# Twelve subtractions moved from VectorE to GpSimd, and one change of issue order, in a spectral-mix kernel

## The chip, the core and the metric

The kernel runs on one core of a Trainium2 chip. The metric is the device time in microseconds (us). The engines are named as the profile names them: PE is TensorE (PEld its weight loads), DVE is VectorE, ACT is ScalarE, POOL is GpSimd, SP is SyncE, which here only issues DMAs. Each engine works through its own instructions in order and waits on semaphores for the others.

## What is computed

Two branches over a token axis of 4096 tokens, 640 channels and batch 2 are mixed by a gate per token: a Fourier branch (`A`) and a gated feed-forward network (`B`, 640 to 1728 to 640).

```python
g = sigmoid((x * gate_w).sum(-1, keepdims=True))
# A: real FFT over the tokens, then per frequency a complex two-layer network in 4 blocks of 160 channels
z = rfft2(x).reshape(B, H, Wf, 4, 160)
hr = relu(zr @ w1[0] - zi @ w1[1] + b1[0]);  hi = relu(zi @ w1[0] + zr @ w1[1] + b1[1])
or_ = hr @ w2[0] - hi @ w2[1] + b2[0];       oi_ = hi @ w2[0] + hr @ w2[1] + b2[1]
a = irfft2(softshrink(or_, 0.01) + 1j * softshrink(oi_, 0.01))
# B
b = (gelu(x @ w_gate) * (x @ w_up)) @ w_down
out = g * a + (1 - g) * b
```

All of it is float32.

## The kernel before

**Operands in two parts.** TensorE multiplies in the type float32r, so each operand is kept as a high part (ACT copies the float32 tile into a float32r tile, `high`, line 276) and a low part (the tile minus its high part, `low`, line 279, a subtraction on DVE unless another engine is given). `split` is the one after the other. A product then is three matmuls: high by high, low by high, high by low.

**Stages.** (1) Up to about 1380 us, three passes over groups of gate and up weight tiles (`groups`), each over 16 tiles of 512 tokens, called pairs (`keys`), compute the hidden layer. In a pair, `quad` saves products by sums of operands: of the four token blocks b11, b12, b21, b22 it also uses the differences t1 = b12 - b11, t2 = b22 - t1, t3 = b22 - b12 and t4 = b21 - t2. These are the tiles `xd`, made at line 441 by `x_prep`. In the first pass each difference is split and its two parts, the tile `xo`, are also stored to DRAM (`xD`) by a DMA that POOL issues at line 468, and the later passes load them. The first pair is made without differences (`plain`), and while TensorE computes it, ACT and DVE prepare the first four weight tiles (`w`, `wt`) and the operands of the second pair; while it computes the second, those of the third. So the second and the third pair are `keys[1]` and `keys[2]`. Small pieces of such preparation are handed out to numbered hooks between the matmul groups (`spread`, `slots`), and the places fix the order of each engine's instructions. The first Fourier step runs in between.

(2) From about 1380 to 1800 us, 64 steps (`steps`, S = 64), each one block of one chunk of frequencies. At a step i the loop issues `mlp1` of step i (first layer), `mlp2` of step i-1 (second layer), and the first inverse step `inv1` of step i-2 where that closes a pair of blocks. `mlp1` makes most of its output `h` at once and hands back a function, `rest_of`, for the last 32 channels (tiles `hl`, lines 926 to 928); the loop calls it, as `more`, behind `mlp2`. `mlp2` evicts its two PSUM banks with an ACT instruction into `m` (line 951) and a DVE instruction into `y` (line 952). `y_split` splits `y` into `ys`.

(3) From about 1800 us, 32 steps of the last inverse Fourier step (`inv2`) and of the down projection (`down`), which mixes and stores the output. The operands of `inv2` are loaded by `c_load` into `s2` and split by `c_split` into the tiles `s2s`; those of `down` are loaded by `h_load` into `hraw`, and `h_s3` subtracts two of them on POOL (line 1145).

**What orders the passage from (2) to (3).** The table `fin` lists what is issued at the end of each of the last steps of stage 2. At S-4 stands `c_load` of the first inverse operands, at S-2 the first `h_load`, and at S-1 `c_split(0)`, the first `h_op` and `h_s3`. At i = S, `mlp2` of the last step needs what `rest_of` made at S-1, and `inv2(0)` comes behind it.

The lines that the change and the prediction touch: 276 (high parts, ACT), 279 (low parts), 441 (differences), 468 (DMA of a difference's parts), 509 (copies out of PSUM in `quad`), 869 and 870 (high and low part of `h`), 909 (`kc`), 923, 926, 927 and 928 (the rest of the first layer), 951 and 952 (second layer out), 1145 (`h_s3`).

Of the kernel before, what the change touches and what calls it, by code (L numbers as in the profile page):

```python
# [213 lines left out]
def spectral_mix_kernel(ctx: ExitStack, tc: tile.TileContext, a):  # L214
    nc = tc.nc
# [26 lines left out]
    def small(shape, dt=F32, name="small"):  # L242
        return pool.tile(shape, dt, name=name, tag="small", bufs=18)
# [31 lines left out]
    def high(dst, src, scale=1.0):  # L275
        nc.scalar.activation(dst, src, AF.Copy, scale=scale)  # L276

    def low(dst, src, hi, eng=nc.vector):
        eng.tensor_sub(dst, src, hi.bitcast(F32))  # L279

    def split(dst_h, dst_l, src, eng=nc.vector):

        high(dst_h, src)
        low(dst_l, src, dst_h, eng)
# [8 lines left out]
    def mms(dst, ops):  # L293
        for i, (l, r) in enumerate(ops):
            nc.tensor.matmul(dst, l, r, start=i == 0, stop=i == len(ops) - 1)  # L295
# [130 lines left out]
    def x_prep(key, k, eng=nc.vector):  # L426

        name = XNAMES[k]
        kept = int(name[1]) - 1 if name in ("t1", "t2", "t3", "t4") else None

        def src():
            d = XT[key]
            if not made(key) and kept is not None:
                m = mid([P, 2, 512], F32R, name="xo")
                ld(m.rearrange("p h n -> p (h n)").bitcast(F32), xD[key[1]][:, kept])
                XO.setdefault(key, {})[name] = [m[:, h] for h in range(2)]
                return
            for n, p, q in (("t1", "b12", "b11"), ("t2", "b22", "t1"), ("t3", "b22", "b12"), ("t4", "b21", "t2")):
                if n not in d and (n == name or (n, name) == ("t1", "t2")):
                    d[n] = small([P, 512], name="xd")  # L440
                    nc.vector.tensor_sub(d[n], d[p], d[q])  # L441
            if name == "t5":
                d[name] = small([P, 256], name="xd")
                nc.vector.tensor_sub(d[name], d["k4"][:, :256], d["k4"][:, 256:])
            return d[name]

        def hi(copy=high):
            if not made(key) and kept is not None:
                return
            if name == "t5":  # L450
                if not T5:
                    T5.append(mid([P, 2, 2, 256], F32R, name="xo"))
                t = [T5[0][:, keys.index(key) % 2, h] for h in range(2)]
            else:
                m = mid([P, 2, 512], F32R, name="xo")
                t = [m[:, h] for h in range(2)]
                if kept is not None:
                    XM[key, name] = m
            XO.setdefault(key, {})[name] = t
            copy(t[0], XT[key][name])  # L460

        def lo():
            if not made(key) and kept is not None:
                return
            t = XO[key][name]
            low(t[1], XT[key][name], t[0], eng)
            if kept is not None:
                nc.gpsimd.dma_start(xD[key[1]][:, kept],
                                    XM.pop((key, name)).rearrange("p h n -> p (h n)").bitcast(F32))
        return [src, hi, lo]  # L470
# [401 lines left out]
    def mlp1(b, c, n, sums):  # L872
        F = width(b, c)
        z, (sh, sl) = Z.pop((b, c, n))
        w, wl = W1[n], W1L[n]
        t1, t2 = ZL1[b, c], ZL2[b, c]

        part = lambda k: (w[:, k:k + P], w[:, LOW1 + k:LOW1 + k + P])
        wl = wl.rearrange("p h c -> p (h c)")


        def group(dst, m):
            r = 1 - m
            wh, wlo = part(OUT1[m])
            mms(dst, [(wh, z[0][:, r]), (wh, z[1][:, r]), (wlo, z[0][:, r]),
                      (wl[:, P * m:P * m + P], t1[:, n, :F]), (wl[:t2.shape[0], 384 + P * m:512 + P * m], t2[:, n, :F])])

        def last(dst):

            for r in range(2):  # L890
                k = LAST1[r]
                nc.tensor.matmul(dst, w[:, k:k + P], z[0][:, r], start=r == 0, stop=False, skip_group_check=True)  # L892
                nc.tensor.matmul(dst, w[:, k:k + P], z[1][:, r], start=False, stop=False, skip_group_check=True)  # L893
            nc.tensor.matmul(dst, wl[:, 256:384], t1[:, n, :F], start=False, stop=True, skip_group_check=True)  # L894
        h = two(b, c, "h")
        if wide(b, c):
            if n < 2:
                x = small([P, 2, CW], F32R, name="hl")
                nc.gpsimd.memset(x[64:66, 1].bitcast(F32), 1.0)
                HW[n] = x[:, 0], x[:66, 1]  # L900
            hA, hB = HW[n % 2]
        else:
            hA, hB = hl1[n % 2], hl2[n % 2]
        H[b, c, n] = (h, hA, hB)
        pk = bank()
        wh, wlo = part(OUT1["k"])
        mms(pk[:, :F], [(wh, sh[:, :F]), (wh, sl[:, :F]), (wlo, sh[:, :F])])
        kc, hs = part_of(b, c, 1), (small if wide(b, c) else mid)([P, 2, F], name="hs")
        nc.scalar.activation(kc[:, :F], pk[:, :F], AF.Copy)
        pm = [bank()] * 2 if F == CH else [bank(), bank()]  # L910
        for r in range(2):
            d = pm[r][:, r * CH:(r + 1) * CH] if F == CH else pm[r][:, :F]
            group(d, r)
        for r in range(2):
            d = pm[r][:, r * CH:(r + 1) * CH] if F == CH else pm[r][:, :F]
            nc.vector.tensor_add(hs[:, r, :F], d, kc[:, :F])
        sums()
        relu_split(h[0], h[1], hs)
        pl = bank()
        last(pl[:, :F])  # L920
        hs = part_of(b, c, 2)[:64]
        nc.scalar.activation(hs, pl[64:, :F], AF.Copy)
        nc.vector.scalar_tensor_tensor(hs, pl[:64, :F], b1r[:, n:n + 1], hs, op0=OP.add, op1=OP.add)

        def rest_of():
            nc.scalar.activation(hB[:64, :F], hs, AF.Relu)
            nc.scalar.activation(hA[:64, :F], hs, AF.Relu)
            nc.vector.scalar_tensor_tensor(hA[64:, :F], hs, 0.0, hB[:64, :F].bitcast(F32), op0=OP.max,
                                           op1=OP.subtract)
        return rest_of  # L930
# [189 lines left out]
            ld(raw, dr(scr2[b], na * P * 2 * D + r * D, [[2 * D, P], [1, D]]))  # L1120
            S2[i].append(raw)

    def c_split(i):
        m = [mid([P, 1024], F32R, name="s2s") for k in range(3)]
        raws, S2[i] = S2[i], {}
        for n, k in enumerate((0, 2, 1, 3)):
            h, l = (m[e if n < 3 else 2][:, o:o + 320] for e, o in ((0, 16 + 320 * (n % 3)), (1, 352 if n > 2 else 32 + 320 * n)))
            split(h, l, raws[k // 2][:, 320 * (k % 2):320 * (k % 2) + 320])
            S2[i][k] = h, l

    def h_load(i, part):
# [179 lines left out]
    keys = [(gr, tp) for gr in range(3) for tp in ([1, 2, 3, 4, 0, *range(5, 16)] if gr == 1 else range(16))]  # L1311
# [76 lines left out]
    for k, (b, n2) in enumerate(a_seq):  # L1388
        i, j = steps_a[k]
# [31 lines left out]
    for i, key in enumerate(keys):  # L1421
# [16 lines left out]
        for j, t in enumerate(quads):  # L1438
# [10 lines left out]
            n = len(late)  # L1449
# [19 lines left out]
    S = len(steps)  # L1469
# [11 lines left out]
    def events(i, j):  # L1481
        for f, *args in todo.get((i, j), []):
            f(*args)
    wl = lambda part, *js: [(wd_load, j, part) for j in js]
# [6 lines left out]
           S - 5: wl(0, 3, 4, 5),  # L1491
           S - 4: [(c_load, 0), *wl(1, 0, 1)],
           S - 3: [(v_load, 1)],
           S - 2: [(h_load, 0, 0), *wl(1, 2), (h_load, 0, 1)],
           S - 1: [(c_split, 0), (h_op, 0, "a11"), *wl(1, 3, 4, 5), *wl(0, 6), (h_s3, 0, nc.gpsimd), (c_load, 1)],
           S: [(h_s2, 0), (h_op, 0, "s2"), (c_split, 1)],
           S + 1: [*wl(1, 6), *wl(3, 0, 3, 6), *wl(4, 4, 5), *wl(5, 4, 6), (wd_later,), (h_s1, 0)]}
    for i in range(S + 2):
        events(i, 0)
        flush()  # L1500
        if i < S:
            events(i, 1)
            if i + 1 < S:
                sums = main_z(*steps[i + 1]) if i else ahead_z
                if steps[i + 1][2] == 3:
                    sc_pop(*steps[i + 1][:2])
            more = mlp1(*steps[i], sums if i + 1 < S else lambda: None)
        if 0 <= i - 1 < S:
            mlp2(*steps[i - 1])
        if i < S:  # L1510
            more()
        if 0 <= i - 2 < S and steps[i - 2][2] % 2:
            inv1(steps[i - 2][0], steps[i - 2][1], steps[i - 2][2] // 2)
            if wide(*steps[i - 2][:2]) and steps[i - 2][2] == 3:
                HW.clear()
                WT.clear()
        if 0 <= i - 1 < S:
            b, c, n = steps[i - 1]
            if n % 2:
                y_split(b, c, n // 2)  # L1520
            if i == S:
                uu.update(inv2(0))
        for f, *args in fin.get(i, []):
            f(*args)
# [4 lines left out]
    for i in range(len(c_seq)):  # L1529
        n = i + 1 if i + 1 < len(c_seq) else None  # L1530
# [60 lines left out]
```

## Time and profile before

| | us |
|---|---|
| median of 3 runs (lowest, highest) | 2536.0 (2535.12, 2536.41) |
| the profiled execution's own time | 2535.42 |
| its span, first to last instruction | 2533.7 |
| PE busy | 2527.2 |
| DVE busy | 2052.9 |
| ACT busy | 1492.7 |
| POOL busy | 372.4 |

A row of a timeline reads: start in us from the span's start, length in us, engine, line, operation, output <- inputs by the program's names with buffer numbers left out, shapes, how many, and in brackets the idle time of the engine before it with what ended it. Equal instructions that follow each other are merged, and their times then overlap a little at the joints. The granted TensorE clock was 1.0 over the whole profiled execution.

### The profile page before, as it was taken

To read this page: it belongs to the slowest core of one execution; us is meant where nothing else is said; L and a number is where in the kernel's file an instruction comes from. 1 tells how busy PE (TensorE), PEld (TensorE's weight loads), DVE (VectorE), ACT (ScalarE), POOL (GpSimd) and SP (SyncE) were. 2 spreads that over 40 slices of the span, in tenths; PEclk is the share of its full clock that TensorE was granted. 3 is DMA by queue.
4 is the path that set the end of the run, shared out by engine and by line. 5 is a ranking of instruction groups with operands and counts; after the bars stand their busy time and mean duration, and the time that the engine had idled before them with its cause. 6 is when DMAs were issued, how large, how long until landed. Compare 5 with 4: busy or idle time off the path is not lost.

```text
span 2533.7 us, 54552 instructions
## 1 busy us (share of the span) xinstructions
PE 2527.2 (100%) x20299; PEld 2522.9 (100%) x20299; DVE 2052.9 (81%) x4218; ACT 1492.7 (59%) x3494; POOL 372.4 (15%) x379
## 2 busy tenths in 40 slices
PE   9999999999999999999999999999999999999999
PEld 9999999999999999999999999999999999999999
DVE  7878767777777767766667788888999999899998
ACT  6655555666665655655556788787644444444443
POOL 0000000000000000000003111111133333333332
PEclk9999999999999999999999999999999999999999
DMA  6566647676767677766767354548744444344432
GB/s 231 195 214 197 212 169 234 203 240 210 223 204 253 192 227 226 232 219 209 225 224 229 121 166 141 169 144 263 288 146 150 156 157 139 134 151 157 154 130 103
DMA packets 345982, 483.77 MB, mean 191 GB/s; under 512 B 24748, under 2 KB 221996, under 8 KB 345716
## 3 DMA queue, kind: packets, MB, share of 16 engines
q1 hardware_dynamic: 330884, 438.47, 54.2%
q0 software_dynamic: 14832, 41.82, 4.6%
q8 instruction: 160, 2.62, 0.4%
q14 instruction: 106, 0.87, 0.1%
HBM read 300.55 MB, written 179.64 MB: 190 GB/s over the span
## 4 chain that ended last, share of the span: by engine, by line
PE 96%; DVE 2%; DMA 1%; ACT 1%; issue 0%; SPq 0%; DVEq 0%; ACTq 0%
PE bank L483 54%; PE bank L1234 22%; PE bank L295 14%; PE bank L811 3%; PE bank L645 1%; PE bank L892 1%; PE bank L893 1%; DMA wraw<-in_wgu_dram 0%; DVE w L279 0%; DVE xo L279 0%; PE bank L894 0%; DVE xd L441 0%; DMA xraw<-in_xT_dram 0%; DVE uu L1239 0%; DVE h L554 0%
## 5 line engine op out<-in xcount | busy, mean ns | idle before, releaser
L483 PE MATMUL bank<-xo,w 128*128 128x256 f32 x11676 | 1351.0, 277 | 0.7 <-ACT u L509 0.6
L483 PEld LDWEIGHTS bank<-xo,w 128*128 128x128 f32 x11676 | 1342.2, 188 | 1.7 <-ACT u L509 1.3
L1234 PE MATMUL bank<-wx,ho 128*128 128x320 f32 x3844 | 560.6, 306 | 0.0
L1234 PEld LDWEIGHTS bank<-wx,ho 128*128 128x128 f32 x3844 | 557.1, 188 | 0.0
L509 ACT ACTIVATE u<-bank 128x256 f32<-128x256 f32 x408 | 156.6, 384 | 253.4 <-PE bank L483 248.3
L279 DVE TENSOR_TENSOR ho<-hraw,ho 128x640 fp32r<-128x640 f32 (+3 forms) x384 | 273.8, 754 | 21.4 <-ACT ho L276 18.4
L276 ACT ACTIVATE ho<-hraw 128x640 fp32r<-128x640 f32 x320 | 166.8, 571 | 91.5 <-PE bank L1234 66.0
L509 ACT ACTIVATE p<-bank 128x256 f32<-128x256 f32 x204 | 78.6, 385 | 148.4 <-PE bank L483 61.9
L279 DVE TENSOR_TENSOR xo<-xraw,xo 128x512 fp32r<-128x512 f32 x209 | 143.2, 686 | 23.9 <-ACT xo L276 23.2
L542 DVE TENSOR_TENSOR u<-bank,u 128x256 f32<-128x256 f32 x204 | 85.9, 421 | 89.2 <-ACT u L509 86.6
L279 DVE TENSOR_TENSOR xs<-xr,xs 64x640 fp32r<-64x640 f32 x128 | 104.9, 820 | 58.1 <-ACT xs L276 55.6
L295 PE MATMUL bank<-wm,h 128*128 128x320 f32 (+1 forms) x792 | 137.7, 309 | 0.0
L276 ACT ACTIVATE xo<-xraw 128x512 fp32r<-128x512 f32 x209 | 131.0, 627 | 6.1 <-DMA xraw<-in_xT_dram 4.3
L551 DVE TENSOR_TENSOR u<-bank,u 128x256 f32<-128x256 f32 x204 | 85.5, 419 | 60.0 <-PE bank L483 59.3
L647 DVE TENSOR_TENSOR as<-bank,as 64x320 f32<-64x320 f32 x256 | 113.7, 483 | 24.9 <-ACT as L646 23.7
L295 PEld LDWEIGHTS bank<-wm,h 128*128 128x128 f32 (+1 forms) x792 | 117.9, 185 | 1.4
L598 POOL MEMSET h<- 64x512 f32 x16 | 8.4, 522 | 749.8 <-PE bank L645 437.5
L483 PE MATMUL bank<-wx,ho 128*128 128x320 f32 x764 | 116.3, 307 | 0.0
L525 DVE TENSOR_TENSOR p<-bank,p 128x256 f32<-128x256 f32 x204 | 86.6, 424 | 36.5 <-PE bank L483 31.9
L483 PEld LDWEIGHTS bank<-wx,ho 128*128 128x128 f32 x764 | 112.1, 188 | 0.0
L276 ACT ACTIVATE ho<-hs 128x640 fp32r<-128x640 f32 (+1 forms) x128 | 69.0, 570 | 70.2 <-DVE ho L279 51.1
L646 ACT ACTIVATE as<-bank 64x320 f32<-64x320 f32 x256 | 96.8, 427 | 16.4 <-PE bank L645 13.9
(168 smaller groups left out, 3669.6 us busy)
## 6 DMA issues: line engine op xcount, KB each, us to landing
xo<-xD SPq DMA_DIRECT2D x124, 512.0 KB
xraw<-in_xT_dram SPq DMA_DIRECT2D x225, 256.0 KB
hD<-h SPq DMA_DIRECT2D x224, 256.0 KB
hraw<-hD SPq DMA_DIRECT2D x128, 320.0 KB
xD<-xo POOLq DMA_DIRECT2D x64, 512.0 KB, 4.3
sc<-scr SPq DMA_DIRECT2D x65, 320.0 KB
xr<-in_x_dram SPq DMA_DIRECT2D x64, 320.0 KB
scr<-as SPq DMA_DIRECT2D x64, 320.0 KB
```

Of the source, the lines that this page charges most:

```text
L276: nc.scalar.activation(dst, src, AF.Copy, scale=scale)
L279: eng.tensor_sub(dst, src, hi.bitcast(F32))
L295: nc.tensor.matmul(dst, l, r, start=i == 0, stop=i == len(ops) - 1)
L483: nc.tensor.matmul(dst, l, r, start=first and i == 0, stop=i == len(ops) - 1, skip_group_check=True)
L509: copy = lambda d, s_: nc.scalar.activation(d, s_, AF.Copy)
L525: nc.vector.tensor_add(p1, A, p1)
L542: nc.vector.tensor_add(u4, C, u4)
L551: nc.vector.tensor_add(u2, C, u2)
L646: nc.scalar.activation(stg[hi, cs], pa[lo, :320], AF.Copy)
L647: nc.vector.tensor_add(stg[hi, cs], pa[hi, :320], stg[hi, cs])
L811: nc.tensor.matmul(pz[:, kp * P:(kp + 1) * P], SC[b, c, kp][:, o:o + P], ft, start=True, stop=True)
L1234: nc.tensor.matmul((X, Y)[k], *op, start=n[k] == 0 and not (more and k), stop=n[k] == tot[k] - 1, skip_group_check=True)
```

## The change

Three edits. The differences t1 to t4 of the second and the third pair (eight subtractions of 128x512) are computed on POOL; their high and low parts stay on ACT and DVE. `c_split(0)` is issued one step earlier, at S-2 ahead of `h_load`, and its four low parts (128x320) are on POOL; its high parts stay on ACT. At step S-1 alone, the rest of the first layer is issued ahead of `mlp2`, and not behind it.

```diff
             for n, p, q in (("t1", "b12", "b11"), ("t2", "b22", "t1"), ("t3", "b22", "b12"), ("t4", "b21", "t2")):
                 if n not in d and (n == name or (n, name) == ("t1", "t2")):
                     d[n] = small([P, 512], name="xd")
-                    nc.vector.tensor_sub(d[n], d[p], d[q])
+                    (nc.gpsimd if key in keys[1:3] else nc.vector).tensor_sub(d[n], d[p], d[q])
...
-    def c_split(i):
+    def c_split(i, eng=nc.vector):
...
-            split(h, l, raws[k // 2][:, 320 * (k % 2):320 * (k % 2) + 320])
+            split(h, l, raws[k // 2][:, 320 * (k % 2):320 * (k % 2) + 320], eng)
...
-           S - 2: [(h_load, 0, 0), *wl(1, 2), (h_load, 0, 1)],
-           S - 1: [(c_split, 0), (h_op, 0, "a11"), *wl(1, 3, 4, 5), *wl(0, 6), (h_s3, 0, nc.gpsimd), (c_load, 1)],
+           S - 2: [(c_split, 0, nc.gpsimd), (h_load, 0, 0), *wl(1, 2), (h_load, 0, 1)],
+           S - 1: [(h_op, 0, "a11"), *wl(1, 3, 4, 5), *wl(0, 6), (h_s3, 0, nc.gpsimd), (c_load, 1)],
...
             more = mlp1(*steps[i], sums if i + 1 < S else lambda: None)
+        if i == S - 1:
+            more()
         if 0 <= i - 1 < S:
             mlp2(*steps[i - 1])
-        if i < S:
+        if i < S - 1:
             more()
```

On POOL at the start of the program, the subtractions come to stand between the DMAs that store the differences' parts. The rows with a minus are before, those with a plus are now.

```order
 L239 MEMSET gap 128x112
-L468 DMA xD_89<-xo 128x1024 x4
+L441 ISA
+L441 TENSOR_TENSOR xd<-xraw 128x512
+L468 DMA xD_89<-xo 128x1024
+L441 TENSOR_TENSOR xd<-xraw 128x512
+L441 TENSOR_TENSOR xd<-xraw,xd 128x512
+L468 DMA xD_89<-xo 128x1024 x2
+L441 TENSOR_TENSOR xd<-xraw,xd 128x512
+L468 DMA xD_89<-xo 128x1024
+L441 TENSOR_TENSOR xd<-xraw 128x512
```

The four differences of the second pair stand in the order t3, t1, t2, t4. Each DMA waits for a low part that DVE makes, so t1 and t2 now stand behind the storing of t3, and t4 behind that of t2 and t1. The first of the third pair follows the last DMA of the second.

On ACT at the end of stage 2, step S-1 before (the tiles: `kc` and `hs` of the first layer, `hl` its rest, `m` of the second layer, `is` of the first inverse step, `s2s` the first inverse operands):

```order
L909 ACTIVATE kc<-bank 128x256
L869 ACTIVATE h<-hs 128x512
L922 ACTIVATE hs<-bank 64x256
L951 ACTIVATE m<-bank,neg2lam 128x320 x2
L926 ACTIVATE hl_20268<-hs 64x256
L927 ACTIVATE hl_20267<-hs 64x256
L987 ACTIVATE is<-bank 128x320 x2
L276 ACTIVATE s2s<-s_26169 128x320
L276 ACTIVATE s2s<-s_26171 128x320
L276 ACTIVATE s2s<-s_26169 128x320
L276 ACTIVATE s2s<-s_26171 128x320
```

and with the change:

```order
L276 ACTIVATE s2s<-s_26169 128x320
L276 ACTIVATE s2s<-s_26171 128x320
L276 ACTIVATE s2s<-s_26169 128x320
L276 ACTIVATE s2s<-s_26171 128x320
L909 ACTIVATE kc<-bank 128x256
L869 ACTIVATE h<-hs 128x512
L922 ACTIVATE hs<-bank 64x256
L926 ACTIVATE hl_20268<-hs 64x256
L927 ACTIVATE hl_20267<-hs 64x256
L951 ACTIVATE m<-bank,neg2lam 128x320 x2
L987 ACTIVATE is<-bank 128x320 x2
```

The four high parts of `s2s` moved from behind the step's work to ahead of it, and the two `m` from ahead of the two `hl` to behind them.

On POOL at the same place, with the change:

```order
L1007 DMA v<-in_v_dram 128x256
L279 TENSOR_TENSOR s2s<-s_26169,s2s 128x320
L279 TENSOR_TENSOR s2s<-s_26171,s2s 128x320
L279 TENSOR_TENSOR s2s<-s_26169,s2s 128x320
L279 TENSOR_TENSOR s2s<-s_26171,s2s 128x320
L1145 TENSOR_TENSOR hraw<-hraw 128x640
L1145 TENSOR_TENSOR hraw<-hraw 128x256
```

The four low parts are new here. Before, `h_s3` (line 1145) followed the DMA directly.

## The prediction, made before the result was known

> **What bounds the kernel now.** I read the page's busy times first, then PE's waits, then the two places that the change touches.
>
> ```profile
> PE 2527.2 (100%) x20299; PEld 2522.9 (100%) x20299; DVE 2052.9 (81%) x4218; ACT 1492.7 (59%) x3494; POOL 372.4 (15%) x379
> PE bank L1344 <- DVE zero L1340: 1.2, 1, 1.2
> PE bank L295 <- ACT is L987: 0.7, 1, 0.7
> PE bank L483 <- ACT u L509: 0.6, 2, 0.5
> ```
>
> PE is busy for 2527.2 of 2533.7 us and all its waits add up to 2.5 us. The first lies at the very end, out of the change's reach; the second is the passage into the last stage, the third is in the start. The change removes no work from PE, so it can win only these small waits, and whatever it makes late on PE is paid in full. I look at the start.
>
> ```profile
> 18.00:57.00 39.00, 38.52 (x335) 38.10 (x335) 38.52 (x95) 23.63 (x62) 4.12 (x8) 1.00 0.59 186
> 18.00:57.00 39.00, 5.38 (x8) 1.00 0.59 186
> 18.00:57.00 39.00, 6.18 (x13) 1.00 0.59 186
> 66.80 21.56 PE bank L483 x190
> 13.85 38.09 PE L483 MATMUL bank<-xo,w 128*128 128x256 f32 x330
> 52.42 9.81 PE L483 MATMUL bank<-xo,w 128*128 128x256 f32 x84 [0.48 <-ACT u L509]
> ```
>
> The first three rows are the window from 18 to 57 us: all engines (PE, PEld, DVE, ACT, POOL), then line 441 alone (the eight subtractions, 0.67 us each), then DVE's operations that read a PSUM bank. DVE is as full as PE: 38.52 of 39 us. It is therefore a second bound, and a delay in its queue reaches PE. How much PE loses there: from 66.80 on, 190 matmuls take 21.56 us, 0.1135 each; at that rate 330 would take 37.45, and they took 38.09. With the 0.48 us idle before 52.42 the start costs PE **1.1 us**.
>
> ```profile
> 17.68 0.69 DVE L587 TENSOR_TENSOR h<-bank,gelu 128x512 f32<-128x512 f32 x1 [4.86 <-ACT gelu L586]
> 20.96 0.68 DVE L441 TENSOR_TENSOR xd<-xraw 128x512 f32<-128x512 f32 x1
> 21.56 0.42 DVE L339 TENSOR_TENSOR wt<-wraw 128x256 f32<-128x256 f32 x1
> 39.38 0.41 DVE L345 TENSOR_TENSOR wt<-wraw 128x256 f32<-128x256 f32 x1
> 50.74 0.69 DVE L441 TENSOR_TENSOR xd<-xraw,xd 128x512 f32<-128x512 f32 x1
> 39.83 1.34 ACT L276 ACTIVATE w<-wt 128x512 fp32r<-128x512 f32 x4 [1.05 <-DVE wt L345]
> 41.60 0.36 ACT L509 ACTIVATE p<-bank 128x256 f32<-128x256 f32 x1
> 51.46 0.63 ACT L276 ACTIVATE xo<-xd 128x512 fp32r<-128x512 f32 x1 [1.65 <-DVE xd L441]
> 52.00 0.37 ACT L509 ACTIVATE u<-bank 128x256 f32<-128x256 f32 x1
> ```
>
> The way from DVE to PE is seen twice. DVE's `wt` at 39.38 releases ACT's high parts at 39.83, behind which ACT's copy out of PSUM at 41.60 is queued. DVE's difference at 50.74 releases ACT's high part at 51.46, behind that stands the copy `u` at 52.00, and PE resumes at 52.42. Both times PE waits for a PSUM copy that stands on ACT behind an operand that DVE made late.
>
> **Edit 1, eight subtractions to POOL.** What leaves DVE: from 20.96 to the next start at 21.56, 0.60 us each. What comes to POOL has no row of its size; two neighbours:
>
> ```profile
> L712 POOL TENSOR_TENSOR raw<-raw 128x128 f32<-128x128 f32 x4 | 1.8, 456 | 2.3 <-DMA raw<-in_w1m_dram 2.2 <-PE bank L483 0.2
> L279 POOL TENSOR_TENSOR ys<-y,ys 128x640 fp32r<-128x640 f32 x29 | 45.7, 1576 | 316.4 <-ACT ys L276 285.6 <-issue 22.4 <-PE bank L295 8.5
> ```
>
> Between 0.456 us for 128 columns and 1.576 for 640, a line gives 1.30 for 512 and 0.88 for 320. Whether DVE goes on meanwhile is the question that decides; these rows of the last stage bear on it:
>
> ```profile
> 1856.36 1.15 DVE L279 TENSOR_TENSOR ho<-hraw,ho 128x640 fp32r<-128x640 f32 x2
> 1826.12 2.54 DVE L279 TENSOR_TENSOR ho<-hraw,ho 128x640 fp32r<-128x640 f32 x2 [0.33 <-ACT ho L276]
> 1826.64 2.62 POOL L1145 TENSOR_TENSOR hraw<-hraw 128x640 f32<-128x640 f32 x2 [27.54 <-DMA hraw<-hD]
> 1861.62 4.89 DVE L279 TENSOR_TENSOR ho<-hraw,ho 128x128 fp32r<-128x128 f32 x1
> 1861.86 2.27 POOL L1145 TENSOR_TENSOR hraw<-hraw 128x640 f32<-128x640 f32 x2
> 1864.09 2.27 POOL L1152 TENSOR_TENSOR hs<-hraw 128x640 f32<-128x640 f32 x2
> ```
>
> Two subtractions that take DVE 1.15 us alone took 2.54 while POOL subtracted; and a small one, begun at 1861.62 while POOL was still issuing a DMA, was not done before POOL's four operations were, 4.89 us later. A DVE operation with both inputs in SBUF and a POOL subtraction do not run side by side; one stands while the other works. [...] By one instruction at a time the first pair of rows is explained; the 4.89 us are four instructions, and there the measurement says that POOL can keep its turn. [...]
>
> So each moved subtraction saves DVE 0.60 and stops it for up to 1.30, unless DVE idles or reads PSUM just then. Seven of the eight stand before PE's wait at 52.42 (the eighth, the third pair's t4, at 56 us). The second pair's first, t3, can run in DVE's 4.86 us of idle ahead of 17.68, since its inputs are loaded for the other parts anyway: it costs nothing. The lag by then is 6 x 1.30 - 7 x 0.60 = 3.6 us if every block bites; 6.18 of the 38.52 us are spent on PSUM operands, so 16% of the time nothing is blocked, which gives 0.84 x 7.8 - 4.2 = 2.4. I take **+3.0** at 52.42, where DVE's delay is passed to PE by the way shown; a part of it comes already at 42 us, where t1, t2 and t4 have gone before. It isn't won back later, since a late PE stays late. DMAs on POOL's queue (line 468) now wait behind the subtractions, at most 1.30 each, and store what the second pass reads hundreds of us on: nothing. Bounds: -1.1 (the start's whole loss vanishes) and 8 x (1.30 - 0.60) = +5.6.
>
> **Edits 2 and 3, the passage.**
>
> ```profile
> 1796.60 0.63 ACT L869 ACTIVATE h<-hs 128x512 fp32r<-128x512 f32 x1 [1.40 <-DVE hs L916]
> 1798.93 0.42 ACT L926 ACTIVATE hl<-hs 64x256 fp32r<-64x256 f32 x1 [0.32 <-DVE hs L923]
> 1800.19 1.54 ACT L276 ACTIVATE s2s<-s 128x320 fp32r<-128x320 f32 x4
> 1795.81 0.75 DVE L916 TENSOR_TENSOR hs<-bank,kc 128x256 f32<-128x256 f32 x2
> 1797.26 1.24 DVE L870 SCALAR_TENSOR_TENSOR h<-hs,h 128x512 fp32r<-128x512 f32 x1 [0.70 <-ACT h L869]
> 1798.82 0.87 DVE L952 SCALAR_TENSOR_TENSOR y<-bank,m 128x320 f32<-128x320 f32 x2
> 1799.72 0.42 DVE L928 SCALAR_TENSOR_TENSOR hl<-hs,hl 64x256 fp32r<-64x256 f32 x1
> 1796.39 2.71 POOL L1145 TENSOR_TENSOR hraw<-hraw 128x640 f32<-128x640 f32 x2 [19.17 <-DMA hraw<-hD]
> 1794.83 0.36 ACT L909 ACTIVATE kc<-bank 128x256 f32<-128x256 f32 x1
> 1800.29 0.53 PE L295 MATMUL bank<-wl,hl 128*128 128x320 f32 x2 [0.73 <-ACT is L987]
> 1796.67 1.90 PE L295 MATMUL bank<-ys,i 128*128 128x320 f32 x12
> 1805.34 2.20 PE L295 MATMUL bank<-ys,i 128*128 128x320 f32 x12
> ```
>
> PE at 1800.29 needs `hl`, whose last part ends at 1800.14 (1799.72 + 0.42); `is` was only the later of the records. Edit 3 takes the two `y` (0.87) from ahead of it: -0.9 on DVE, where ACT's two `hl` don't end later. Edit 2 puts four high parts (1.5 us) ahead of `kc`: it then ends at 1796.7, not 1795.2, and line 916 starts there, not at 1795.81: +0.9, carried by ACT's `h` to line 870, now at 1798.1. Line 870 and line 928 have two SBUF inputs, and POOL now has four low parts of 0.88 from about 1795.9 to 1799.4, then `h_s3`, so far running from 1796.39. If they take turns, line 870 waits about 0.35 for the third low part, and line 928 most of `h_s3`'s first, 1.2 (of 1.58, the row of 640 columns). Sum: -0.9 + 0.9 + 0.35 + 1.2 = +1.6. DVE no longer makes the four lows, so the `ys` that PE met late at 1805.34 (2.20 us for what took 1.90 at 1796.67) comes in time: -0.3. Together **+1.3**. Bounds: -1.0 (0.73 and 0.30 vanish) and +2.7 (below).
>
> **Sum.** 2535.42 + 3.0 + 1.3 = 2539.7 for a profiled execution; that of before lies 0.6 below its median of 2536.0, so against the medians I forecast **2540.2**. About 0.2%, 5.1 us, is what a measurement of this kernel can tell from no change.
>
> **Rivals.** (A) The relief works: POOL runs early, where DVE doesn't need its inputs, DVE's 5.38 us become free and the waits vanish. At best 2536.0 - 1.1 - 1.0 = 2533.9; with half of it, 2535. For it: POOL idles nearly all the time, and in many places it and DVE only alternate. Against it: DVE has no free half microsecond in the window to let POOL through. (B) POOL keeps its turn over the whole row at the passage, as at 1861.62: line 870 stands until four lows (3.5) and `h_s3` (2.3, as 1861.86) are through, from 1795.9 to 1801.7; then 870, 923 and 928 follow, 1.4 us, to 1803.1 in place of 1800.14: +3.0, with the -0.3 above +2.7. Time 2536.0 + 3.0 + 2.7 = 2541.7, slower by more than the bound. It decides as soon as POOL goes through two or more operations without letting line 870 in between. For it: the row of 4.89; against it: 2.54 at 1826.12. (C) The change doesn't do what it says: the subtractions, behind DMAs that wait for low parts of DVE (so t1 and t2 behind the storing of t3), fall where DVE waits anyway, and all comes out even, 2536.
>
> **How the numbers follow.** Forecast 0.50, with a range of its own of 2538.5 to 2542; A 0.20, B 0.25, C 0.05. The range for 8 in 10 runs from 2534.5, which leaves half of A out, to 2543.0, above which lie B with the start's upper bound and the tail of the forecast. Faster than 2530.9 would need twice what the waits hold: 0.02. Slower than 2541.1: four fifths of B (0.20) and a fifth of the forecast (0.11): 0.31. Within: 0.67.
>
> **What would show it.** In the changed kernel's timeline, line 441's rows on POOL of 1.3 us each, and in the same microseconds DVE rows with two SBUF inputs of 1.5 to 2.5 us in place of 0.7; PE idle around 42 and 52 us by 2 to 3 us in all; the copy `u` of 52.00 at 55. At the passage, `kc` near 1.5 us later against its neighbours, line 870 or 928 stretched beside POOL's four lows, PE's `hl` wait of 0.73 grown to about 2.3, the `ys` row back at 1.90. If DVE's rows keep their lengths beside POOL's, edit 1 is wrong at its root and A holds. If line 870 stands for over 3 us, B does. If PE's gaps are the same as before at both places, C.

## The result, and the profile after

The changed kernel takes 2542.14 us (median of 14 runs, 2540.0 to 2544.4), against 2536.52 for the kernel before in as many runs beside it (2535.12 to 2538.24): a ratio of 1.0021, 95% interval 1.0013 to 1.0030, 5.6 us more (3.3 to 7.6 by the interval). The forecast was 2540.2; the median lies just above the forecast's own range (2538.5 to 2542) and inside the range for 8 in 10 runs.

The profiled execution took 2543.02 us, its span is 2541.3, 7.6 more than before. Its page, and PE's waits:

```profile
PE 2530.1 (100%) x20299; PEld 2525.1 (99%) x20299; DVE 2054.3 (81%) x4206; ACT 1492.8 (59%) x3494; POOL 386.8 (15%) x391
...
PE bank L483 <- ACT p L509: 1.7, 1, 1.7
PE bank L295 <- DVE hl L928: 1.6, 1, 1.6
PE bank L483 <- ACT u L509: 1.1, 2, 0.9
```

POOL has 12 instructions more, 14.4 us. DVE has 12 fewer and is busy 1.4 us longer: it lost work and gained standing time. PE's waits in the start grew from 0.5 to 2.6 us, the one at the passage from 0.7 to 1.6. In PE's timeline:

```profile
44.58 10.16 PE L483 MATMUL bank<-xo,w 128*128 128x256 f32 x84 [1.69 <-ACT p L509]
55.69 10.83 PE L483 MATMUL bank<-xo,w 128*128 128x256 f32 x93 [0.95 <-ACT u L509]
...
1808.04 0.53 PE L295 MATMUL bank<-wl,hl 128*128 128x320 f32 x2 [1.60 <-DVE hl L928]
1813.09 1.90 PE L295 MATMUL bank<-ys,i 128*128 128x320 f32 x12
```

The copies of which PE waits at 44.58 and 55.69 are the two of before (42.0 and 52.42). Behind the second, PE is 55.69 - 52.42 = 3.27 us late. What happened to DVE stands in its groups over the start: first the four that changed, in the window from 18 to 60 us of the changed kernel, then the same groups before, from 18 to 57 (busy us in total, mean ns of one).

```profile
L279 DVE TENSOR_TENSOR w<-wt,w 128x128 fp32r<-128x128 f32 x16 | 6.3, 432 | 0.0
L279 DVE TENSOR_TENSOR w<-wt,w 128x512 fp32r<-128x512 f32 x4 | 4.5, 1118 | 0.1
L279 DVE TENSOR_TENSOR w<-wraw,w 128x640 fp32r<-128x640 f32 x4 | 4.3, 1086 | 0.0
L345 DVE TENSOR_TENSOR wt<-wraw 128x256 f32<-128x256 f32 x4 | 2.7, 674 | 0.0
```

```profile
L279 DVE TENSOR_TENSOR w<-wt,w 128x128 fp32r<-128x128 f32 x16 | 4.0, 283 | 0.0
L279 DVE TENSOR_TENSOR w<-wraw,w 128x640 fp32r<-128x640 f32 x4 | 3.2, 818 | 0.0
L279 DVE TENSOR_TENSOR w<-wt,w 128x512 fp32r<-128x512 f32 x4 | 2.7, 687 | 0.0
L345 DVE TENSOR_TENSOR wt<-wraw 128x256 f32<-128x256 f32 x4 | 1.7, 417 | 0.0
```

The same instructions, on the same data, take 17.8 us and took 11.6: 6.2 us of standing. One place, in the timelines of POOL, DVE and ACT:

```profile
24.42 1.31 POOL L441 TENSOR_TENSOR xd<-xraw 128x512 f32<-128x512 f32 x1
25.81 1.63 POOL L441 TENSOR_TENSOR xd<-xraw,xd 128x512 f32<-128x512 f32 x1
36.98 1.51 POOL L441 TENSOR_TENSOR xd<-xraw,xd 128x512 f32<-128x512 f32 x1
23.89 2.40 DVE L279 TENSOR_TENSOR w<-wt,w 128x512 fp32r<-128x512 f32 x1
26.21 1.91 DVE L279 TENSOR_TENSOR w<-wraw,w 128x640 fp32r<-128x640 f32 x1
39.19 0.69 DVE L279 TENSOR_TENSOR xo<-xd,xo 128x512 fp32r<-128x512 f32 x1 [1.25 <-ACT xo L276]
38.52 0.63 ACT L276 ACTIVATE xo<-xd 128x512 fp32r<-128x512 f32 x1 [1.36 <-POOL xd L441]
```

The row of 2.40 (alone 0.69) is done only at 26.29, 0.56 us behind POOL's first subtraction (25.73); the next, of 1.91, begins at 26.21 and is done 0.68 us behind POOL's second (27.44). They take turns here, one instruction each (POOL is done at 25.73, DVE at 26.29, POOL at 27.44, DVE at 28.12). It was not always the later one that stood: POOL's second began at 25.81, 0.40 us ahead of the row of 1.91, but the row of 2.40 began at 23.89, 0.53 us ahead of POOL's first, and stood for it all the same. The last two rows show a second loss: t4 comes from POOL only at 38.5, ACT waits 1.36 us for it, DVE 1.25 for ACT.

PE's second wait, at 55.69, has a way of its own (POOL twice, ACT):

```profile
51.30 0.57 POOL L468 DMA_DIRECT2D xD<-xo  x1 [9.22 <-DVE xo L279]
53.27 1.43 POOL L441 TENSOR_TENSOR xd<-xraw,xd 128x512 f32<-128x512 f32 x1
54.74 0.63 ACT L276 ACTIVATE xo<-xd 128x512 fp32r<-128x512 f32 x1 [2.96 <-POOL xd L441]
```

The low part of the third pair's t3 starts on DVE at 50.31 (48.35 before): DVE is 1.96 us late there. Its store is issued by POOL at 51.30, and t1 and t2 stand behind it, so t2 is done at 54.70, 4.39 us after the start of that low part. Before, on DVE, t2 was done at 51.43, 3.08 us after it. ACT waits 2.96 us for t2, and PE for ACT's copy `u` behind it. Of the 3.27 us, 1.96 are DVE's lag, and 1.31 are the longer way of t1 and t2 through POOL. DVE stands once more in the row from 51.79 on, for 2.4 of the 6.2 us, but beside this way, and PE does not wait for that.

The passage, in the timelines of ACT, DVE and POOL:

```profile
1802.78 0.37 ACT L909 ACTIVATE kc<-bank 128x256 f32<-128x256 f32 x1
1805.81 0.42 ACT L926 ACTIVATE hl<-hs 64x256 fp32r<-64x256 f32 x1 [0.74 <-DVE hs L923]
1803.18 0.76 DVE L916 TENSOR_TENSOR hs<-bank,kc 128x256 f32<-128x256 f32 x2 [0.77 <-ACT kc L909]
1804.69 0.69 DVE L870 SCALAR_TENSOR_TENSOR h<-hs,h 128x512 fp32r<-128x512 f32 x1 [0.76 <-ACT h L869]
1806.26 1.64 DVE L928 SCALAR_TENSOR_TENSOR hl<-hs,hl 64x256 fp32r<-64x256 f32 x1 [0.48 <-ACT hl L926]
1801.89 4.23 POOL L279 TENSOR_TENSOR s2s<-s,s2s 128x320 fp32r<-128x320 f32 x4 [18.15 <-ACT s2s L276]
1806.08 2.41 POOL L1145 TENSOR_TENSOR hraw<-hraw 128x640 f32<-128x640 f32 x2
```

PE is 6.48 us late when it gets here, so 1802.78 is 1796.30 of before: `kc` comes 1.47 us later, line 916 0.89, line 870 0.95. Line 870 is not held at all (0.69; it took 1.24 before, when `h_s3` ran beside it). Line 928 takes 1.64 in place of 0.42: it stands 1.2 us for `h_s3`, which starts at 1806.08. It ends at 1807.90, PE goes on at 1808.04.

### The profile page after: what moved, and what is told of

The parts are those of the page before. It is cut to its first block, busy times and chain, and to the rows that moved or that the text cites. A ratio compares the mean times of both kernels' runs of the same rounds, so it can differ in the third digit from the quotient of the medians.

```text
span 2541.3 us, 54564 instructions
## 1 busy us (share of the span) xinstructions
PE 2530.1 (100%) x20299; PEld 2525.1 (99%) x20299; DVE 2054.3 (81%) x4206; ACT 1492.8 (59%) x3494; POOL 386.8 (15%) x391
## 4 chain that ended last, share of the span: by engine, by line
PE 94%; DVE 2%; ACT 1%; DMA 1%; issue 1%; POOL 0%; SPq 0%; DVEq 0%; ACTq 0%; POOLq 0%
PE bank L483 53%; PE bank L1234 22%; PE bank L295 14%; PE bank L811 3%; PE bank L645 1%; PE bank L892 1%; PE bank L893 1%; DMA xraw<-in_xT_dram 0%; DVE w L279 0%; DVE xo L279 0%; PE bank L894 0%; DMA hD<-h 0%; DMA wdf<-wf 0%; POOL xd L441 0%; ACT xo L276 0%
## 5 line engine op out<-in xcount | busy, mean ns | idle before, releaser
L646 ACT ACTIVATE as<-bank 64x320 f32<-64x320 f32 x256 | 96.8, 427 | 16.4 <-PE bank L645 13.9
```

Source lines behind the costliest of these rows:

```text
L646: nc.scalar.activation(stg[hi, cs], pa[lo, :320], AF.Copy)
```

## The experiments

Both traces have the same 20299 matmuls in the same order, so the start of a matmul, less that of the same one in the profile of before, tells how late PE is at any place. This table gives it for all runs (us; the last column is the growth over the passage, 1790 to 1808 on the clock of before).

| kernel | late at 13.9 | late at 60 | growth 370 to 450 | growth, passage | median, or the one run | before beside it |
|---|---|---|---|---|---|---|
| changed | -0.13 | 3.27 | 2.19 | 0.97 | 2542.14 | 2536.52 |
| changed, again (e10) | -0.63 | 3.29 | 0.02 | 1.00 | 2540.19 | 2536.22 |
| edit 1 alone (e1) | -0.25 | 4.31 | 2.18 | 0.41 | 2542.0 | 2537.54 |
| edit 2 alone (e2) | -0.94 | -0.34 | 2.28 | 2.40 | 2538.44 | 2537.54 |
| edit 3 alone (e3) | 0.08 | 0.21 | -0.01 | 1.31 | 2537.57 | 2537.54 |
| idle subtractions (e4) | -0.02 | 2.80 | -0.02 | 0.43 | 2540.15 | 2537.54 |
| edit 1, stores behind (e5) | -0.17 | 3.04 | 0.00 | 0.01 | 2540.78 | 2537.24 |
| idle memsets (e6) | -0.47 | -0.33 | 2.19 | 0.08 | 2537.48 | 2537.24 |
| early split on DVE (e7) | 0.62 | 0.96 | 2.29 | 4.94 | 2540.86 | 2537.24 |
| late split on POOL (e8) | -0.35 | -0.05 | 2.28 | 1.34 | 2537.42 | 2537.24 |
| before, again (e9) | -0.26 | 0.05 | -0.02 | 0.30 | 2536.26 | 2536.22 |
| edit 1 in pieces (e11) | 0.04 | 9.76 | 0.00 | 0.30 | 2543.75 | 2536.22 |
| negation on ACT (e12) | 1.81 | 2.27 | 0.01 | 0.50 | 2536.7 | 2536.22 |

Where nothing was changed in the start, PE loses 0.1 to 0.6 us more between 13.9 and 60 than in the profile of before, and where nothing was changed at the passage, 0.0 to 0.5: that much is chance, and the first profile a good one. At the passage this lies in line 870: beside `h_s3` it takes 1.24 us in the profile of before, 1.52 in e9, 1.65 in e1 and 1.69 in e3. Counted from 13.9 us, the start loses 3.4 (changed), 3.9 (e10), 4.6 (e1), 3.2 (e5) and 2.8 (e4). The growth of 2.2 us from 370 to 450 comes in six of these executions, with and without edit 1.

**e1, edit 1 alone**

```diff
-                    nc.vector.tensor_sub(d[n], d[p], d[q])
+                    (nc.gpsimd if key in keys[1:3] else nc.vector).tensor_sub(d[n], d[p], d[q])
```

> The kernel before with edit 1 alone (the eight differences on POOL). Theory 1, the start is where most is lost and DVE stands while POOL subtracts: PE's second and third wait of the start (1.69 and 0.95 us in the changed kernel) are there again, PE at 56 us is 3.0 to 3.5 us later than before, the passage is as before (wait of 0.73 us), the time 2539 to 2541. Rival, most of the loss is in the passage: PE is less than 1 us late at 56 us, the time within 1 us of before.

2542.0 us, ratio 1.0017 (1.0008 to 1.0026). The start is late by 4.31, the wait at the passage is the old 0.7. Theory 1 holds, its 3.0 to 3.5 us fell short; edit 1 carries most of the loss. Why more than the 3.3 of the whole change, which has the same start? POOL, then DVE:

```profile
17.94 1.82 POOL L441 TENSOR_TENSOR xd<-xraw 128x512 f32<-128x512 f32 x1 [16.98 <-DMA xraw<-in_xT_dram]
18.53 2.65 DVE L279 TENSOR_TENSOR w<-wraw,w 128x640 fp32r<-128x640 f32 x2
```

The second pair's t3 ran at 17.05 in the changed kernel, while DVE idled and then read PSUM. Here its input landed later, it began at 17.94, and DVE's two rows took 2.65 us in place of 1.55. So this difference is free in one execution and costs 1.1 us of DVE's time in another.

**e2, edit 2 alone**

```diff
-           S - 2: [(h_load, 0, 0), *wl(1, 2), (h_load, 0, 1)],
-           S - 1: [(c_split, 0), (h_op, 0, "a11"),
+           S - 2: [(c_split, 0, nc.gpsimd), (h_load, 0, 0), *wl(1, 2), (h_load, 0, 1)],
+           S - 1: [(h_op, 0, "a11"),
```

(The rows of S - 1 are shown up to what changes, and `c_split` hands its engine on, as in the change.)

> The kernel before with edit 2 alone (first inverse operands split one step earlier, low parts on POOL, the rest of layer 1 in its old place behind the second layer). Theory 1, edit 2 costs and edit 3 gives back a part of it: start as before, PE loses 1.5 to 2.5 us at the passage against before, more than the 1.1 of both edits together; the time 2538 to 2539. Rival, edit 3 is what hurts: PE loses nothing or gains up to 0.5 us at the passage.

Ratio 1.0002 (0.9993 to 1.0011), not to be told from before. In the profile the passage grows by 2.40, as theory 1 says, but a part of it is something else. PE's timeline, and a window of it (PE, PEld, DVE, ACT, POOL, then the granted clock):

```profile
1803.96 0.87 PE L295 MATMUL bank<-wl,hl 128*128 128x320 f32 x2 [1.61 <-ACT ho L276]
1804.63 1.80 PE L295 MATMUL bank<-wm,h 128*128 128x320 f32 x6
1804.00:1806.00 2.00, 2.00 (x8) 2.00 (x9) 2.00 (x5) 0.65 (x2) 0.40 (x1) 0.50 1.00 415
```

The wait is as long as in the changed kernel, 1.61 (it names `ho`, which is only the later of the records: `hl` was done 0.01 us ahead of it), but behind it the granted clock is 0.50, and six matmuls take 1.80 us, not 1.04. From 1800.29 to 1801.97 of before PE loses another 1.4 us (3.67 to 5.05 late) by it. Without it edit 2 costs about 1.0, no less and no more than edits 2 and 3 together; that edit 3 gives back a part, as theory 1 has it, is not shown.

**e3, edit 3 alone**

```diff
+        if i == S - 1:
+            more()
         if 0 <= i - 1 < S:
             mlp2(*steps[i - 1])
-        if i < S:
+        if i < S - 1:
             more()
```

> The kernel before with edit 3 alone (the rest of layer 1 ahead of the second layer at the last step). Theory 1: PE's wait of 0.73 us for the rest of layer 1 shrinks to 0.1 to 0.5, nothing else moves, the time 0 to 0.6 us below before. Rival, the second layer's eviction is now late: PE waits 0.3 to 1 us more for the operands ys made from it, the time up to 1 us above before.

Ratio 1.0003 (0.9994 to 1.0012). The rival is right in the profile: PE loses 1.31 at the passage, 0.43 of it at 1798.6 us, as e1 and e4 do with the passage unchanged.

```profile
1800.93 0.95 ACT L951 ACTIVATE m<-bank,neg2lam 128x320 f32<-128x320 f32 x2
1807.96 1.72 PE L295 MATMUL bank<-ys,i 128*128 128x320 f32 x10 [0.30 <-DVE ys L279]
```

The evictions `m` (1797.66 before, here 0.8 us of lateness on top) stand at 1800.93, 2.4 us later by the same clock, behind two `hl` that wait for line 923; the operands `ys` at the end of that chain are late. Edit 3 on its own saves the wait for `hl` in part (0.4 is left of 0.73) and pays more than that back; the times do not tell it from before.

**e4, idle subtractions, and e6, idle memsets**

```diff
-                    nc.vector.tensor_sub(d[n], d[p], d[q])
+                    nc.vector.tensor_sub(d[n], d[p], d[q]); [nc.gpsimd.tensor_sub(gap[1], d[p][:, :112], d[q][:, :112]) for r in range(3 * (key in keys[1:3]))]
```

and in e6 `nc.gpsimd.memset(gap[1], 0.0)`, six times, in the place of the three. `gap` is a tile that nothing reads.

> The kernel before, all its subtractions still on DVE; at the eight places POOL makes three subtractions of 128x112 of the same inputs into a tile that nothing reads (about 1.3 us each place, by 0.456 us for 128 columns). Theory 1, POOL's subtraction stops DVE: DVE saves nothing and loses up to 1.3 us per place, so PE at 56 us is 4 to 7 us later than before. Rival, the place on POOL's queue is what makes the differences late: nothing waits for these, PE is as before within 0.5 us.

> The kernel before, all its subtractions on DVE; at the eight places POOL makes six memsets of 128x112, which read nothing, into a tile that nothing reads. Theory 1, it is POOL's reading that stops DVE: PE at 60 us is within 0.5 us of before, no DVE row is stretched. Rival, any work of POOL stops DVE or delays its stores: PE is 1.5 to 3 us later, as with the idle subtractions (2.8).

PE is 2.80 us late at 60 us with the subtractions, and not late with the memsets. Timelines, first of e4 (POOL, DVE), then of e6 (POOL, PE):

```profile
25.32 2.17 POOL L441 TENSOR_TENSOR gap<-xraw 128x112 f32<-128x112 f32 x3
24.80 0.87 DVE L279 TENSOR_TENSOR w<-wt,w 128x512 fp32r<-128x512 f32 x1
25.60 1.05 DVE L279 TENSOR_TENSOR w<-wraw,w 128x640 fp32r<-128x640 f32 x1
```

```profile
24.75 2.95 POOL L441 MEMSET gap<- 128x112 f32 x12
13.38 49.54 PE L483 MATMUL bank<-xo,w 128*128 128x256 f32 x423
```

Twelve memsets keep POOL busy for 2.95 us, no row of DVE in the start is over 0.1 us longer than before, and PE runs from 13.38 to 62.9 without one wait worth a row. Three subtractions that nothing waits for stretch DVE's rows from 0.69 to 0.87 and from 0.82 to 1.05. So in the start POOL's subtractions, which read SBUF, stop DVE, and these memsets, which only write, do not; neither POOL's being busy nor its place in a queue does it there by itself. That a memset never stops DVE is not shown: in the changed kernel DVE's line 716 (128x64) took 1.02 us from 1356.60 on, beside POOL's memset of line 779 (1356.58 to 1357.56), and 0.24 at 1365.59. The size was below the 4 to 7 us expected: one such POOL instruction, under 0.5 us, holds DVE by only some 0.2 (3.05 us over the whole start), and POOL is held as well (three take 2.17 us at 25.32, and 1.44 at 17.22).

**e5, the stores behind the fourth difference** (on top of edit 1)

```diff
-                nc.gpsimd.dma_start(xD[key[1]][:, kept],
-                                    XM.pop((key, name)).rearrange("p h n -> p (h n)").bitcast(F32))
+                stores.append((xD[key[1]][:, kept], XM.pop((key, name)).rearrange("p h n -> p (h n)").bitcast(F32)))
+                [nc.gpsimd.dma_start(*stores.pop(0)) for r in stores[:] if key not in keys[1:3] or name == "t4"]
```

> Edit 1 alone, and the four DMAs that store a pair's differences stand on POOL's queue behind the fourth difference of the pair, not between them. Theory 1, the shared way to SBUF decides: POOL's subtractions start earlier but stop DVE as before, PE at 60 us is 2 to 4 us later than before the change (4.3 with edit 1 alone). Rival, the queue decides, since each subtraction stands behind a DMA that waits for DVE: PE at 60 us is within 0.7 us of before the change.

Ratio 1.0014 (1.0005 to 1.0023); PE 3.04 us late at 60. POOL, then PE:

```profile
20.61 1.31 POOL L441 TENSOR_TENSOR xd<-xraw,xd 128x512 f32<-128x512 f32 x1 [0.52 <-DMA hD<-h]
51.97 6.28 PE L483 MATMUL bank<-xo,w 128*128 128x256 f32 x52 [2.50 <-ACT p L509]
```

The difference t2 is made at 20.61, not 25.81, and PE still waits 2.50 us, here for DVE alone: the copy `p` stands on ACT behind high parts that wait for line 345 on DVE, at 49.55 (45.73 before). Ahead of it seven rows of DVE stood, 7.0 us in all. So standing by itself costs about as much as edit 1 does with the stores in between (3.04 against 3.27 and 3.29). Of the shared way to SBUF in theory 1 the traces show these standing rows and no more. What the stores in the queue cost is not shown by this: moving them also moves POOL's subtractions beside other rows of DVE.

**e11, edit 1 in pieces**

```diff
-                    nc.vector.tensor_sub(d[n], d[p], d[q])
+                    [(nc.gpsimd if key in keys[1:3] else nc.vector).tensor_sub(d[n][:, c], d[p][:, c], d[q][:, c]) for c in ([slice(128 * r, 128 * r + 128) for r in range(4)] if key in keys[1:3] else [slice(0, 512)])]
```

> Edit 1 alone, each difference on POOL as four subtractions of 128x128 in place of one of 128x512. Theory 1a, DVE stands for a whole POOL instruction, so shorter ones let it in between: rows of DVE are stretched by 0.2 to 0.5 us and not by 1.1 to 2, PE at 60 us is 1.5 to 3.0 us later than before (4.3 and 3.3 with whole ones). Theory 1b, only the sum of POOL's reading time counts: PE is 3.3 to 4.5 us later, as with whole ones.

Ratio 1.0029 (1.0018 to 1.0040), PE 9.76 us late at 60: neither theory. The timelines of POOL, ACT and PE:

```profile
25.39 2.78 POOL L441 TENSOR_TENSOR xd<-xraw 128x128 f32<-128x128 f32 x4
58.24 0.63 ACT L276 ACTIVATE xo<-xd 128x512 fp32r<-128x512 f32 x1 [4.79 <-POOL xd L441]
59.19 7.00 PE L483 MATMUL bank<-xo,w 128*128 128x256 f32 x34 [2.79 <-ACT u L509]
```

In turns POOL is held as well: a difference takes 2.78 us, ACT waits 4.79 for two of them, PE 2.79 for ACT's copy behind; and then 34 matmuls take 7.00 us (0.21 each, at a clock of 0.50) for what takes 3.9 at 0.1135. Of the 9.76 us, 3.0 come at this clock; PE was 6.8 late when it went on at 59.19. DVE's rows were stretched less, most by 0.2 to 0.3, as 1a says, but what came late now was the difference itself. The two losses trade against each other.

**e7 and e8, the split of the inverse operands: only earlier, and only on POOL**

```diff
-           S - 2: [(h_load, 0, 0),
-           S - 1: [(c_split, 0), (h_op, 0, "a11"),
+           S - 2: [(c_split, 0), (h_load, 0, 0),
+           S - 1: [(h_op, 0, "a11"),
```

```diff
-           S - 1: [(c_split, 0),
+           S - 1: [(c_split, 0, nc.gpsimd),
```

(The rows are shown up to what changes; in e8 `c_split` hands its engine on, as in the change.)

> The split of the first inverse operands one step earlier, its low parts on DVE, and nothing else changed: no new POOL work. Theory 1, at the passage the four high parts ahead of kc on ACT and not POOL cost the most: PE is 1.0 to 2.2 us later over the passage (from 1790 to 1815 us), with its wait for hl near 2 us. Rival, POOL's low parts cost it: PE loses less than 0.5 us there.

> The split of the first inverse operands in its old place, its low parts on POOL. Theory 1, POOL's four low parts (0.88 us each, in place of 0.40 on DVE) are late for the matmuls with s2s, which follow at once: PE loses 0.5 to 2 us in the row of s2s matmuls, none ahead of it. Rival, DVE is what is late at the passage and is now free: PE gains up to 0.5 us.

e7: ratio 1.0013 (1.0004 to 1.0022). DVE, then PE:

```profile
1799.62 3.06 DVE L279 TENSOR_TENSOR s2s<-s,s2s 128x320 fp32r<-128x320 f32 x4
1804.12 0.41 PE L295 MATMUL bank<-wm,h 128*128 128x320 f32 x1 [1.78 <-ACT h L869]
```

The four low parts stand ahead of line 916 on DVE and, with `h_s3` on POOL beside them, take 3.06 us (1.69 before); PE waits 1.78 for `h`, then 0.73 for `hl`, and from 1805.8 on goes at a granted clock of 0.50. It loses 4.94 us, over twice the 2.2 at the upper end of theory 1; 2.4 of them come at half the clock, 2.5 ahead of that. e8: ratio 1.0000 (0.9992 to 1.0009). PE, then POOL:

```profile
1805.32 0.70 PE L295 MATMUL bank<-s2s,v 128*128 128x320 f32 x3 [0.77 <-POOL s2s L279]
1802.07 4.21 POOL L279 TENSOR_TENSOR s2s<-s,s2s 128x320 fp32r<-128x320 f32 x4 [23.07 <-PE bank L295]
```

As theory 1 says, PE catches up with POOL within the row of `s2s` matmuls (0.77 + 0.31 us of waits). In these profiles both halves of edit 2 hurt alone (the times show it for e7 only), and each covers a part of the other's loss: the earlier place gives POOL the time that it needs, and POOL keeps the four low parts off DVE's path.

**e9 and e10, the two kernels once more**

> The kernel before once more, for how much one profiled execution differs from another. If the profile of before is typical, PE's rows lie within 0.5 us of it at every place; if not, this shows where the unchanged kernel itself scatters (the passage: 0 to 1.2 us more, as the two kernels with an unchanged passage had, 0.4 and, up to 1830 us, 1.1; slower matmuls from 385 to 440 us: 2.2).

> The changed kernel once more. Theory 1: the loss in the start (3.3 us at 60 us) and at the passage (1.0) is there again within 1 us each, wherever the rest of the 7.6 us falls. Rival: most of the 7.6 us of the first profile was chance, and the start loses less than 1.5.

e9 is within 0.5 us of the profile of before up to the passage, 0.9 late at the end. e10, PE's timeline:

```profile
28.41 14.72 PE L483 MATMUL bank<-xo,w 128*128 128x256 f32 x124 [1.20 <-DVE w L279]
55.72 8.45 PE L483 MATMUL bank<-xo,w 128*128 128x256 f32 x72 [1.29 <-ACT u L509]
1805.19 0.53 PE L295 MATMUL bank<-wl,hl 128*128 128x320 f32 x2 [1.61 <-DVE hl L928]
```

The lateness of 3.3 at 60 us and the passage's 1.0 are there again to 0.1 us. PE waits 1.20 at 28.41 here, and is no later at 60 than in the first profile: the waits that follow end when DVE and POOL are done, however PE stood before. The rest of the first profile's 7.6 us (a further 2.2 from 370 to 450 us, and 0.86 at 1357) is not.

**e12, another relief of DVE**, on the kernel before: the negation at line 359 on ACT.

```diff
-            nc.vector.tensor_scalar(e[:, 1], u[:, 4], -1.0, None, op0=OP.mult)
+            high(e[:, 1], u[:, 4], scale=-1.0) if t in groups[0][:4] else nc.vector.tensor_scalar(e[:, 1], u[:, 4], -1.0, None, op0=OP.mult)
```

> The kernel before, and in the start the four negations of a weight tile (line 359, 0.13 us each from start to start) on ACT instead of DVE: relief of DVE that brings no second reader of SBUF. Theory 1, DVE sets the pace of the start and ACT has room: PE at 60 us is 0.2 to 0.6 us earlier than before, the time not to be told from before. Rival, ACT's copies out of PSUM behind the four are late in turn: PE is up to 0.8 us later.

```profile
15.66 48.57 PE L483 MATMUL bank<-xo,w 128*128 128x256 f32 x411
```

Ratio 1.0000 (0.9990 to 1.0009). PE has no wait worth a row from 15.66 to 64.2 us; but it began 1.8 us later here, so that it asked for its operands later, and matmuls went at 0.118 us (48.57 / 411), not 0.1135. They did so ahead of the first negation too: the 24 of line 572 from 12.83 to 15.66 took 0.118 us each, and the negation stands on ACT behind a high part that needs DVE's line 345, done at 22.49. So the slower pace is not the edit's. ACT's negations read SBUF as DVE's did; DVE's rows beside them and behind them kept their lengths (0.69, 0.68 and 0.82 us at 22.95, 24.49 and 25.09). Whether the negations had a part in the missing waits is open. No version was found that beats the kernel before beyond what can be told.

## Why the prediction was right, point by point

**The bound.** That PE had only a few waits to give, and DVE stood behind them, was right: no part of the change, alone or together, came out faster.

**Edit 1: +3.0 at 52.42, measured 3.27 and 3.29.** The mechanism holds: POOL's subtractions stop DVE, and PE waits for ACT's copies `p` and `u` behind a late operand. e4 and e6 show the stopping apart from queue and dependency, e5 its cost without a late difference. As a sum it fits the first wait. By then three rows of DVE had stood 3.8 us (1.71, 1.09 and 1.03) and DVE had waited 1.25 for t4, less four subtractions of 0.60: 2.7, and PE was 2.57 late. The wait for t4 was missing in the prediction: it counted how long POOL's subtraction stops DVE, not that the result itself comes late to ACT. t4 stopped nothing, as DVE was mostly in line 587, which reads PSUM and kept its 0.69 us.

At the second wait the sum does not describe what happened. The prediction passes DVE's whole lag to PE. The lag on PE's way was 1.96, and 1.31 came from t1 and t2 on POOL behind the store of t3. The prediction had weighed the DMAs that stand behind subtractions, at nothing, but not the subtractions behind DMAs; it named that order only in rival C. The standing, put at 0.84 x 7.8 = 6.6 us and measured as 6.2, is well sized. But 6.2 - 4.2 + 1.25 would also give 3.25, and this is chance: 2.4 of the 6.2 fall beside the second wait's way. So that 3.0 came within 0.3 of the measured values is in part luck. That t3 costs nothing held in both profiles of the changed kernel and not in e1.

**The passage: +1.3, measured 0.97 and 1.00.** `kc` 1.5 later, line 916 0.9 later, 1.2 for `h_s3`'s first on line 928 and the -0.3 on `ys` all came as worked out. Two terms were off. Line 870 was to wait 0.35 and didn't; POOL waited (its four took 4.23 us for 4 x 0.88 = 3.5), and line 870 became 0.55 shorter, as the row of 1.24 before had held a wait for `h_s3` that is now gone. And edit 3 was to bring line 928 forward by 0.9; from the start of line 923 to that of line 928 it is now 0.96 us and was 1.29, so 0.33: ACT's two `hl` and so line 928 wait for line 923, which the working passed over by saying that they "don't end later". Summed on PE's clock: 0.95 (start of line 870) - 0.55 - 0.33 + 1.22 - 0.3 = 1.0. Even the 0.33 is worth nothing here: line 928 ends 0.28 us behind `h_s3`'s first with edit 3 (1807.89 and 1807.61) and without it (e2, 1803.81 and 1803.53), and PE's wait is 1.6 both times. Since executions with the passage unchanged lose up to 0.5 there against the profile of before, the change's own share is between 0.5 and 1.0. That edit 3 costs by itself when the rest of the change isn't there (e3) was not foreseen.

**The sum.** 2539.7 for a profiled execution; the two took 2543.02 and 2540.19. The second lost little besides the start and the passage, and is half a microsecond off. In the first, matmuls were slow for a stretch, which no step of the prediction speaks of (last section). Against the medians the forecast was 1.9 us low. How much of this is that stretch can't be told from times alone.

**The rivals.** A (relief) is refuted by the changed kernel and by e1: DVE's rows did not keep their lengths beside POOL. B (POOL keeps its turn over a row) did not come: rows of DVE get in after each POOL instruction, at 26.2 us, and at the passage line 870 takes its 0.69 us at 1804.69, within POOL's four. C is refuted by the 3.3 us at the start; the order that it named, t1 and t2 behind the storing of t3, is what made 1.31 of them.

## What to carry to other kernels

In this kernel, work moved from a full VectorE to an idle GpSimd was no relief. Beside GpSimd's subtractions, VectorE operations with two SBUF operands stood (2.40 us for one that takes 0.69 alone), while one that reads PSUM kept its 0.69: a moved subtraction took 1.3 us of GpSimd, and seven of them cost more standing (6.2 us) than they saved (4.2). Ask the same of any such move. Count the latency of the result as well as the blocking, and what stands ahead of it on its new queue: t1 and t2, behind a store and on the slower engine (1.30 and 1.43 us there, 0.69 on VectorE), were worth 1.31 of 3.27 us. Cutting the instruction up lowered the blocking (most rows of VectorE were longer by 0.2 to 0.3 us) and raised the latency (2.78 us for a difference), and lost more (6.8 us late against 4.3, and 9.8 with the granted clock of 0.50 behind the wait). Follow the way back from each wait by itself; a sum over the whole start can come out right by chance. Where the whole effect is 0.2%, take the profile of the same kernel twice and compare PE instruction by instruction: 1 us at one place was seen so, which the medians could not tell.

## What the runs showed of the hardware

**Slower matmuls at a full granted clock.** From 387 to 433 us, first the kernel before, then the changed one (PE, PEld, DVE, ACT, POOL, granted clock):

```profile
387.00:433.00 46.00, 46.00 (x408) 46.00 (x407) 33.26 (x93) 26.26 (x71) 0.53 (x1) 1.00 0.73 233
387.00:433.00 46.00, 46.00 (x393) 46.00 (x392) 33.73 (x92) 25.81 (x70) 0.53 (x1) 1.00 0.69 222
```

In the same 46 us PE made 408 matmuls in the one and 393 in the other, busy throughout: 0.1127 and 0.117 us each, while the clock reads 1.00 in both. It cost 2.2 us and is seen in six executions of different kernels at nearly the same place, not in the others. The two paces are not bound to this place: from 14 to 33 us e12 makes 164 matmuls and the profile of before 169, and the profile of before makes 78 in each 9 us from 515 to 533 (0.115 us each) and 89 in the 10 us from 540 to 550 (0.112), all at a clock of 1.00. What decides it is open.

**A wait can cost twice.** The granted clock fell to 0.50 at 1803.8 in e2, within a wait of 1.61 us, for 3.4 us (it is 0.91 over 1803 to 1804, 0.50 up to 1807, 0.88 over 1807 to 1808); at 1805.8 in e7, where the wait of 0.73 begins, 1.7 us behind that of 1.78, for 6.8 us (0.94 over 1804 to 1806, 0.50 up to 1812, 0.85 over 1812 to 1814); and in e11 between 56 and 59, within a wait of 2.79 that lasts from 56.40 to 59.19, up to 65.3 (1.00 up to 56, 0.50 from 59 to 65, 0.93 over 65 to 67). It stayed at 1.00 behind the 1.60 and 1.61 us of the two executions of the changed kernel, and behind waits of 2.50 us in e5 and in e11 (at 46.24). So the length of the wait alone does not decide it, and what does is not shown by these runs.
